# Sliding-window attention and a token-mixing MLP on one core: ScalarE's transpose copies as 4-byte words, part-wise waits, 20 output buffers, and 17 stores held back

## Chip, cores and metric

The kernel runs on one core of one Trainium2 chip. The core's engines are TensorE (PE in the profile, PEld for its weight loads), VectorE (DVE), ScalarE (ACT), GpSimd (POOL) and SyncE (SP), each with a queue of its own that runs in order and waits on semaphores. DMAs are issued from POOL (loads), SP (stores, three of the first loads) and ACT (three first loads, two last stores). The metric is the device time of one execution, in microseconds (us).

## What is computed

The reference, cut to its core. The batch is 8, heads 8, sequence 576, head size 64; all inputs and the output are float32.

```
scores = (q @ k.T) / sqrt(64) - slope[h] * |i - j|      # slope = 2 ** -(h + 1)
mask   = (i - j >= 0) & (i - j < 128)
attn   = softmax(where(mask, scores, -1e9))
x      = (attn @ v), heads side by side                   # (8, 576, 512)
wq, wk = x @ w_q, x @ w_k                                 # (8, 576, 64)
W      = wq @ wk.T / sqrt(64)                             # (8, 576, 576)
out    = relu(W @ x) @ w_out                              # (8, 576, 512)
```

## The kernel before, in words

The work is cut into small operations, and their order on every engine is a table of words, `ORDER` (lines 49 to 118). A word such as `QK2.1.0:P2` is an operation's name and its engine: P is PE, with the PSUM pair (and half) that it writes, A is ACT, D is DVE, G is POOL, S is SP. `Order.follow` reads the table, and the kernel emits each operation in that order (lines 1037 to 1041). A tile framework adds the waits between engines.

The names that this text uses, with batch b, query group g (0 to 3, of 128 rows each; the last 64 rows of a batch are its tail) and half u of the heads:

- Loads on POOL: `Lq`, `Lk`, `Lv`, and `Lt` (the tails of two batches). They read float32 and write float16.
- `TQb`, `TKb.m`, `TTb`, `TJ` on PE transpose q, k and the tails into PSUM as float16; `ETQ`, `ETK`, `ETT`, `EJ` copy the result into the tile `qkT` (two of them, for batch b % 2), on ACT or DVE as the table says.
- `QKb.g.u` on PE makes scores, `EXPb.g.u` on ACT their exponential (line 657), `MULb.g` on DVE multiplies by mask and distance bias (line 672).
- `PVb.t` on PE multiplies by v, `RCb.t` and `Xb.t` on DVE divide by the sums: x, 128 rows at a time (t = 4 is the tail).
- `XTb.i` and `XTT` on PE transpose x; `EXTb.i` and `EXTT` copy it into the tile `xT` or `xTt`, on ACT or DVE.
- The MLP goes by groups of two batches (`GROUPS`): `WQ`, `WK`, `WT`, `G`, `MX` on PE with their evictions `EWQ`, `EWK`, `EWT`, `EG`, `RM`, `RMT`, then `OUTb.st` on PE, `EOb.st` on ACT or DVE (a copy from PSUM into an output buffer `osb`), and `DOb.st`, the store of 256 KB from that buffer. The last block of all, 7.3, is done in two halves, a and b.

Every copy goes through `cp` (lines 250 to 254): `scalar.copy` on ACT (L252 in the profile), `tensor_copy` on DVE (L254). All matmuls are recorded at L240, transposes at L243. Output buffers come from one pool of `OSB = 14` (line 35); the first three loads of q and k use three of them too. An `EO` needs a free buffer, which means that the store which read it has landed. The stores are nearly all on SP's queue, in the order of the table; the first, DO3.3, stands there behind EO3.3, and the stores of groups 0 and 1 (batches 0 to 3) follow it, each between other words.

The framework tracks whole regions of a tile: two operations of different engines that write interleaved pieces of one tile can be made to wait for each other. `apart` (lines 258 to 271) takes such waits away between the two halves of a PSUM pair.

Of the kernel before, what the change touches and what calls it, by code (L numbers as in the profile page):

```python
# [34 lines left out]
OSB = 14  # L35

GROUPS = ((0, 1), (2, 3), (4, 5), (6, 7))

LOGB = ()
# [27 lines left out]
Lk3.3:G QK2.0.1:P1 X1.4:D EXT0.1:D QK2.1.1:P0 Lk3.2:G EXP2.0.1:A TT2:P3 QK2.1.0:P2 ETT2:D
Lv2.1:G EXP2.1.1:A ETT3:D WK0:P10 MUL2.0:D Lv2.2:G EXP2.1.0:A XTT0:P0 QK2.3.0:P3 EXTT0:D
WQ0:P11 Lv2.3:G EWK0:A MUL2.1:D EXP2.3.0:A QK2.3.1:P0 TQ3:P2 Lq4.0:G MUL2.2:D EXP2.3.1:A Lwo0:G
WT0:P10 ETQ3:D PV2.0:P0 EWT0:A Lwo1:G TK3.0:P3 ETK3.0:A G0:P10 RC2.0:D Lk4.1:G X2.0:D MUL2.3:D  # L70
EWQ0:A Lk4.0:G TK3.1:P3 EG0:A QK3.0.0:P0 EXP3.0.0:A Lv3.0:G ETK3.1:D MX0.0:P1 QK3.0.1:P2
RM0.0:D MX0.1:P3 EXP3.0.1:A Lv3.1:G MX0.3:P0 Lq5.01:G RM0.3:D RM0.1:A PV2.1:P1 QK3.1.0:P2
RC2.1:D PV2.2:P3 EXP3.1.0:A X2.1:D MX0.2:P0 RC2.2:D QK3.3.1:P1 RM0.2:A X2.2:D PV2.3:P2 Lq5.02:G
MUL3.0:D QK3.1.1:P3 EXP3.3.1:A XT2.0:P00 PV2.4:P01 RC2.3:D EXP3.1.1:A Lq5.03:G X2.3:D TQ4:P1
RC2.4:D EXT2.0:A X2.4:D QK3.2.1:P3 ETQ4:D OUT0.2:P20 Lq5.00:G EXP3.2.1:A XT2.1:P21 Lv3.2:G
MUL3.1:D EO0.2:A QK3.2.0:P1 TK4.0:P3 Lv3.3:G EXP3.2.0:A QK3.3.0:P0 ETK4.0:D OUT0.1:P20 Lk5.0:G
EXT2.1:D EXP3.3.0:A QK4.0.1:P1 MUL3.2:D QK4.1.1:P3 Lk5.1:G OUT1.3:P21 EXP4.1.1:A Lv3.4:G
MUL3.3:D PV3.0:P0 EO0.1:A PV3.1:P3 Lk4.3:G EXP4.0.1:A OUT1.1:P20 RC3.1:D RC3.0:D X3.1:D Lk4.2:G
EO1.3:A QK4.1.0:P1 X3.0:D TQ5:P3 EXP4.1.0:A Lt2:G MX0.4:P0 XT3.0:P21 ETQ5:D RMT0:A PV3.2:P1
EO1.1:A PV3.3:P0 Lv5.0:G RC3.2:D EXT3.0:A X3.2:D OUT1.2:P20 Lv4.0:G RC3.3:D X3.3:D QK4.0.0:P1  # L80
TK5.0:P3 Lv4.1:G EXP4.0.0:A XT3.1:P21 ETK5.0:D PV3.4:P00 Lk5.3:G EO1.2:A QK5.1.0:P3 RC3.4:D
QK5.0.1:P1 X3.4:D EXP5.1.0:A OUT0.0:P20 Lv4.2:G EXT3.1:D MUL4.0:D EXP5.0.1:A QK5.0.0:P0 Lk5.2:G
TK4.1:P3 OUT0.3:P21 EXP5.0.0:A Lk6.0:G ETK4.1:D TT4:P1 EO0.0:D EO0.3:A Lq6.02:G XTT2:P3
QK5.1.1:P0 ETT5:D ETT4:A OUT1.0:P20 EXTT2:D Lk6.2:G EXP5.1.1:A MUL4.1:D PV4.0:P3 Lk6.1:G
# [6 lines left out]
MX2.0:P3 RC5.1:D PV4.3:P0 Lq7.01:G X5.1:D RM2.0:A QK5.3.1:P2 RC4.3:D TQ6:P1 Lv5.2:G X4.3:D
EXP5.3.1:A MX2.1:P3 ETQ6:D QK5.3.0:P0 Lq7.03:G RM2.1:A XT4.1:P20 Lq7.00:G PV4.4:P21 EXT4.1:D
EXP5.3.0:A TK7.0:P1 QK6.1.0:P3 Lv5.4:G ETK7.0:D OUT3.3:P20 EXP6.1.0:A RC4.4:D Lv5.3:G X4.4:D
QK6.1.1:P1 MUL5.2:D QK6.2.1:P0 QK6.2.0:P3 Lv7.3:G EXP6.1.1:A OUT2.1:P21 Lk7.2:G EXP6.2.0:A
XT5.0:P10 OUT2.3:P11 Lk7.3:G EO2.1:A EXT5.0:D EXP6.2.1:A MUL5.3:D PV5.2:P3 Lv6.2:G OUT2.2:P10
EO3.3:A Lv6.0:G RC5.2:D EO2.3:A DO3.3:S X5.2:D TT6:P2 EO2.2:A TQ7:P0 Lv6.1:G DO0.2:S ETT6:D
QK6.0.1:P3 ETT7:D DO2.1:S QK6.0.0:P1 ETQ7:D Lv6.3:G EXP6.0.1:A PV5.4:P20 DO0.1:S OUT3.2:P21
DO1.3:S Lv6.4:G EXP6.0.0:A RC5.4:D DO1.0:S MUL6.1:D QK6.3.0:P0 Lv7.0:G DO0.0:S PV5.3:P3
EXP6.3.0:A OUT3.1:P10 X5.4:D Lv7.4:G RC5.3:D EO3.2:A X5.3:D Lv7.2:G QK6.3.1:P0 EO3.1:A
QK7.1.0:P2 MUL6.0:D MX2.4:P3 EXP6.3.1:A XT5.1:P11 Lv7.1:G OUT2.0:P10 RMT2:D EXP7.1.0:A EXT5.1:D  # L100
TK7.1:P0 QK7.0.0:P3 EO2.0:A XTT4:P2 MUL6.2:D OUT3.0:P11 EXTT4:A EXP7.0.0:A ETK7.1:D WT4:P10
QK7.1.1:P2 MUL6.3:D EWT4:A QK7.0.1:P3 PV6.0:P0 EXP7.1.1:A WK4:P10 RC6.0:D X6.0:D EXP7.0.1:A
# [57 lines left out]
def kernel(  # L160
# [75 lines left out]
    def hold(i):  # L236
        held.append(i.ins)
# [12 lines left out]
    def cp(eng, out_ap, in_ap):  # L250
        if eng == "ACT":
            hold(nc.scalar.copy(out_ap, in_ap))  # L252
        else:
            hold(nc.vector.tensor_copy(out=out_ap, in_=in_ap))  # L254
# [820 lines left out]
```

## Time and profile before

| | us |
|---|---|
| runs shown | 136.86, 137.61, 137.75 (median 137.61) |
| the profiled execution | 138.33 |
| its span, first to last instruction | 136.6 |
| busy: PE / DVE / ACT / POOL | 124.7 / 114.1 / 107.5 / 86.3 |
| weight loads on PE (PEld) | 79.3 |

The span is what the trace shows; 1.7 us of the profiled execution lie around it. Of an engine's row in a timeline, the first number is the start from the beginning of the span, the second the time, and the brackets hold how long the engine was idle just before and what ended that. In groups of instructions by line, the numbers behind the bar are busy time, mean nanoseconds of one, and idle time ahead of them. A wait for several semaphores is put down to the one that came last.

### The profile page before, as it was taken

How to read it: one execution, taken by the hardware profiler on the slowest of the kernel's cores; microseconds unless marked ns; L12 is line 12 of the kernel's file. 1: busy time of each engine (PE TensorE's matmuls, PEld its weight loads, DVE VectorE, ACT ScalarE, POOL GpSimd, SP SyncE). 2: the span in 40 equal slices, each digit the busy share in tenths (PEclk: the TensorE clock that was granted, in tenths of full speed). 3: DMA queues.
4: the chain of work that ended last, by engine and by line, in shares of the span. 5: the costliest groups of instructions: out<-in, count | busy, mean ns of one | idle time of the engine just before them, and what ended most of it. 6: DMA issues, size and time to landing. Idle time of an engine off the chain costs nothing.

```text
span 136.6 us, 5058 instructions
## 1 busy us (share of the span) xinstructions
PE 124.7 (91%) x2176; PEld 79.3 (58%) x2176; DVE 114.1 (84%) x197; ACT 107.5 (79%) x145; POOL 86.3 (63%) x108
## 2 busy tenths in 40 slices
PE   6889668999999799999999999998999999999980
PEld 2456447676667476575566675564586476643440
DVE  5747979699999999998999999699899999557730
ACT  2579977896898999998999999997999971457030
POOL 7998969599969949899999999996000000000000
PEclk9999965899999999999999999999999999999999
DMA  4999999999999999999999999999999910759894
GB/s 100 216 176 168 157 154 184 160 156 154 151 159 165 196 181 153 157 154 156 155 157 157 153 150 149 150 198 229 240 233 323 321 58 5 236 180 349 257 366 154
DMA packets 105414, 24.97 MB, mean 183 GB/s; under 512 B 95536, under 2 KB 100912, under 8 KB 105392
## 3 DMA queue, kind: packets, MB, share of 16 engines
q0 software_dynamic: 96832, 14.42, 149.0%
q1 hardware_dynamic: 6688, 9.44, 20.5%
q10 hardware_dynamic: 1872, 0.79, 2.2%
q8 instruction: 17, 0.28, 0.8%
q14 instruction: 5, 0.04, 0.1%
HBM read 29.62 MB, written 9.44 MB: 286 GB/s over the span
## 4 chain that ended last, share of the span: by engine, by line
PE 49%; DMA 18%; POOL 10%; DVE 8%; ACT 8%; issue 3%; ACTq 0%; POOLq 0%; DVEq 0%
PE pair L240 41%; DMA natq<-in_q_dram 11%; PE pair L243 8%; DMA natk<-in_k_dram 6%; POOL natk L367 5%; ACT pt L657 4%; DVE qkT L254 2%; DVE pt L672 2%; POOL vt L393 2%; DVE rm L888 1%; DVE x L733 1%; POOL natt L387 1%; ACT qkT L252 1%; POOL natq L371 1%; POOL wqk_sb L455 1%
## 5 line engine op out<-in xcount | busy, mean ns | idle before, releaser
L657 ACT ACTIVATE pt<-pair 128x1024 f16<-128x1024 f32 x64 | 63.1, 1036 | 6.5 <-PE pair L240 6.0
L672 DVE TENSOR_TENSOR pt<-pt,bias 128x2048 f16<-128x2048 f16 x32 | 38.5, 1215 | 0.7 <-ACT pt L657 0.7
L393 POOL DMA_DIRECT2D vt<-in_v_dram x40 | 35.5, 980 | 0.7 <-DMA natq<-in_q_dram 0.4
L240 PE MATMUL pair<-wout_sb,rm 128*128 128x512 f16 (+1 forms) x132 | 31.7, 373 | 0.4 <-ACT osb L252 0.4
L367 POOL DMA_DIRECT2D natk<-in_k_dram x31 | 28.8, 956 | 2.0 <-DMA natq<-in_q_dram 1.5
L240 PEld LDWEIGHTS <-pt 128*128 128x128 f16 (+1 forms) x576 | 19.9, 103 | 6.6 <-issue 2.7
L240 PE MATMUL pair<-vt,pt 128*128 128x65 f16 (+1 forms) x576 | 22.9, 198 | 0.8 <-DVE rm L888 0.5
L240 PE MATMUL pair<-qkT 64*128 64x256 f16 (+2 forms) x320 | 22.6, 253 | 0.9 <-DVE qkT L254 0.5
L252 ACT COPY osb<-pair 128x512 f32<-128x512 f32 (+1 forms) x24 | 14.0, 597 | 11.3 <-PE pair L240 9.7
L733 DVE TENSOR_TENSOR x<-pair,inv 128x512 f16<-128x512 f32 x32 | 21.8, 690 | 0.9
L254 DVE COPY qkT<-pair 128x1024 f16<-128x1024 f16 (+2 forms) x27 | 19.3, 734 | 3.6 <-PE pair L243 3.5
L240 PEld LDWEIGHTS <-rm 128*128 128x128 f16 x132 | 11.4, 97 | 12.5 <-issue 2.7
L240 PEld LDWEIGHTS <-qkT 64*128 64x128 f16 x320 | 11.1, 94 | 8.8 <-issue 5.4
L379 POOL DMA_DIRECT2D natq<-in_q_dram x12 | 11.6, 1005 | 2.1 <-PE pair L240 1.4
L254 DVE COPY osb<-pair 128x512 f32<-128x512 f32 (+1 forms) x13 | 8.7, 667 | 5.1 <-PE pair L240 5.1
L886 ACT ACTIVATE rm<-pair 128x1024 f16<-128x1024 f32 x11 | 11.1, 1046 | 0.5 <-PE pair L240 0.3
L243 PE MATMUL pair<-identh,x 128*128 128x128 f16 x128 | 10.2, 225 | 0.4 <-ACT pt L657 0.4
L243 PEld LDWEIGHTS <-x 128*128 128x128 f16 x128 | 8.0, 100 | 2.7 <-issue 1.6
L240 PE MATMUL pair<-warm 128*128 128x512 f16 x24 | 8.1, 454 | 1.6 <-DVE warm L295 1.2
L254 DVE COPY xT<-pair 128x1024 f16<-128x1024 f16 x11 | 7.5, 685 | 1.9 <-PE pair L243 1.7
L243 PE MATMUL pair<-identh,natk 64*128 64x64 f16 x248 | 7.1, 194 | 2.0 <-DMA natk<-in_k_dram 0.8
L243 PEld LDWEIGHTS <-natk 64*128 64x128 f16 x248 | 5.6, 96 | 4.7 <-issue 2.8
(68 smaller groups left out, 135.9 us busy)
## 6 DMA issues: line engine op xcount, KB each, us to landing
out_dram<-osb SPq DMA_DIRECT2D x30, 256.0 KB, 3.4
vt<-in_v_dram POOLq DMA_DIRECT2D x32, 128.0 KB, 7.5
natk<-in_k_dram POOLq DMA_DIRECT2D x31, 128.0 KB, 6.0
natq<-in_q_dram POOLq DMA_DIRECT2D x4, 512.0 KB, 7.7
natq<-in_q_dram POOLq DMA_DIRECT2D x12, 128.0 KB, 5.6
out_dram<-osb SPq DMA_DIRECT2D x9, 128.0 KB, 2.5
vt<-in_v_dram POOLq DMA_DIRECT2D x8, 64.0 KB, 5.7
natt<-in_q_dram POOLq DMA_DIRECT2D x4, 128.0 KB, 5.6
```

Of the source, the lines that this page charges most:

```text
L240: hold(nc.tensor.matmul(*a, **k))
L243: hold(nc.tensor.transpose(*a))
L252: hold(nc.scalar.copy(out_ap, in_ap))
L254: hold(nc.vector.tensor_copy(out=out_ap, in_=in_ap))
L367: return lambda: nc.gpsimd.dma_start(out=natk(b, n), in_=k[b, :, P * n:P * n + P, :].transpose([1, 0, 2]))
L371: return lambda: nc.gpsimd.dma_start(out=natq_s[b % NQ][r0 // QR:P].rearrange("p h r d -> p h (r d)"), in_=q[b, :, r0:512, :].rearrange("h ...
L379: return lambda: nc.gpsimd.dma_start(out=rows_q(b)[:, r], in_=q[b, :, 0:512, :].rearrange("h (p r) d -> r p h d", r=QR)[r])
L393: return lambda: nc.gpsimd.dma_start(out=vtv(b, t)[:n, :, 0:D], in_=v[b, :, P * t:P * t + n, :].transpose([1, 0, 2]))
L657: nc.scalar.activation(out=pt, in_=two(hold_.bank).rearrange("p e c -> p (e c)"), func=AF.Exp, scale=SCALE)
L672: nc.vector.tensor_tensor(out=pv, in0=pv, in1=bt, op=ALU.mult)
L733: nc.vector.tensor_tensor(out=x_s[b % NX][qt].rearrange("p (g h d) -> p g h d", g=2, h=4), in0=sums(p)[:, :, :, 0:64], in1=box["inv"].unsq ...
L886: hold(nc.scalar.activation(out=out_ap, in_=in_ap, func=AF.Relu, scale=WSCALE))
```

## The change

1. `cp` on ACT: where source and destination are both float16, both are read as float32 words, so that one element holds two values.
2. `parts` is new, and `apart` calls it: for operations that touch `qkT` and `xT` it drops the framework's waits between engines and adds waits for the operations on which this one depends and for the earlier users of its PSUM banks.
3. `OSB` is 20 in place of 14.
4. In `ORDER` the words `DO` of the 17 first stores stand together behind EO3.0, DO3.0 first. Without the words `DO`, the table is the same before and after, word for word.
5. `LOGB`, which was empty, goes, with the branches that it would have switched on.

```diff
-OSB = 14
+OSB = 20
...
-LOGB = ()
...
-EO2.3:A DO3.3:S X5.2:D TT6:P2 EO2.2:A TQ7:P0 Lv6.1:G DO0.2:S ETT6:D
+EO2.3:A X5.2:D TT6:P2 EO2.2:A TQ7:P0 Lv6.1:G ETT6:D QK6.0.1:P3 ETT7:D QK6.0.0:P1 ETQ7:D Lv6.3:G
...
-PV6.1:P2 MUL7.1:D PV6.2:P0 EO3.0:A QK7.3.0:P3 EWK4:A RC6.2:D DO3.0:S RC6.1:D WQ4:P11 X6.2:D
+PV6.2:P0 EO3.0:A DO3.0:S DO0.2:S DO0.1:S DO1.3:S DO1.1:S DO1.2:S DO0.0:S DO0.3:S DO1.0:S DO1.4:S
+DO2.1:S DO3.3:S DO2.3:S DO2.2:S DO3.2:S DO3.1:S DO2.0:S QK7.3.0:P3 EWK4:A RC6.2:D RC6.1:D WQ4:P11
...
     def cp(eng, out_ap, in_ap):
         if eng == "ACT":
+            if out_ap.dtype == F16 and in_ap.dtype == F16:
+                out_ap, in_ap = out_ap.bitcast(FP32), in_ap.bitcast(FP32)
             hold(nc.scalar.copy(out_ap, in_ap))
...
+    PARTS = {"QK": "q", "EF": "q", "EJ": "q", "ETQ": "q", "ETK": "q", "ETT": "q", "EXT": "x"}
+    user, freed = {}, {}
+
+    def parts(op):
+
+        halves = [(op.bank[0], h) for h in range(2)] if op.banks == 2 else [op.bank] if op.banks else []
+        before = [o for x in halves for o in (user.get(x), *freed.get(x, ()))]
+        for x in halves:
+            user[x], freed[x] = op, []
+        for f in op.frees:
+            for h in range(2):
+                freed.setdefault((f.bank[0], h), []).append(op)
+        if op.kind in PARTS:
+            tile_ = PARTS[op.kind] + str(op.batch % (2 if PARTS[op.kind] == "q" else NX))
+            near = [d for d in (*op.deps, *before) if d is not None and d.insts]
+            keep = [i for d in near for i in d.insts]
+            for d in near:
+                if d.eng != op.eng:
+                    tc.add_manual_dep(held[0], d.insts[-1].name,
+                                      mybir.DependencyInfo(mybir.DependencyClass.Sync, mybir.DependencyReason.DATA),
+                                      reason="the parts it uses")
+            for i in held:
+                for e in KIND:
+                    if e != op.eng:
+                        tc.declare_no_dep(i, group=f"parts{tile_}{e}", keep=keep, reason="another part of the tile")
+                tc.add_to_no_dep_group(f"parts{tile_}{op.eng}", i)
+
     def apart(op):
...
         op.insts = list(held)
+        parts(op)
...
-            ps = two((bi or o).bank)
+            ps = two(o.bank)
```

**On ACT, from EXP6.3.0 to EXTT4.** The rows are, in turn, EXP6.3.0, EO3.2, EO3.1, EXP6.3.1, EXP7.1.0, EO2.0 and EXTT4, with the semaphores that each waits for; DMAHW0 to DMAHW7 tell of landed loads and stores of SP and ACT. Before:

```order
L657 ACTIVATE pt_101<-pair_140 128x1024 [waits DVE_49,PE_49]
L252 COPY osb<-pair_142 128x512 [waits DMAHW5_49,DMAHW3_49]
L252 COPY osb<-pair_141 128x512 [waits DMAHW6_49,PE_49,Activation_49]
L657 ACTIVATE pt_101<-pair_140 128x1024 [waits PE_49]
L657 ACTIVATE pt_103<-pair_142 128x1024 [waits DVE_49,PE_49]
L252 COPY osb<-pair_141 128x512 [waits DMAHW7_49,PE_49]
L252 COPY xTt_126<-pair_142 128x512 [waits PE_49]
```

And with the change:

```order
L654 ACTIVATE pt_99<-pair_138 128x1024 [waits DVE_49,PE_49]
L245 COPY osb<-pair_140 128x512
L245 COPY osb<-pair_139 128x512 [waits PE_49]
L654 ACTIVATE pt_99<-pair_138 128x1024 [waits PE_49]
L654 ACTIVATE pt_101<-pair_140 128x1024 [waits DVE_49,PE_49,Activation_49]
L245 COPY osb<-pair_139 128x512 [waits PE_49]
L245 COPY xTt_124<-pair_140 128x256 [waits PE_49]
```

The order of the instructions is the same. The three copies into `osb` no longer wait for a DMA, and the copy into `xTt` has 256 elements of a partition in place of 512.

**On SP, the first eight stores.** The number behind `osb` tells the buffers' uses apart; before, they are those of DO3.3, DO0.2, DO2.1, DO0.1, DO1.3, DO1.0, DO0.0 and DO3.0:

```order
L993 DMA out_0_dram<-osb_2050 128x512
L993 DMA out_0_dram<-osb_1221 128x512
L993 DMA out_0_dram<-osb_2024 128x512
L993 DMA out_0_dram<-osb_1286 128x512
L993 DMA out_0_dram<-osb_1316 128x512
L993 DMA out_0_dram<-osb_1577 128x512
L993 DMA out_0_dram<-osb_1537 128x512
L993 DMA out_0_dram<-osb_2384 128x512
```

With the change they are those of DO3.0, DO0.2, DO0.1, DO1.3, DO1.1, DO1.2, DO0.0 and DO0.3:

```order
L987 DMA out_0_dram<-osb_2375 128x512
L987 DMA out_0_dram<-osb_1219 128x512
L987 DMA out_0_dram<-osb_1284 128x512
L987 DMA out_0_dram<-osb_1314 128x512
L987 DMA out_0_dram<-osb_1390 128x512
L987 DMA out_0_dram<-osb_1469 128x512
L987 DMA out_0_dram<-osb_1535 128x512
L987 DMA out_0_dram<-osb_1537 128x512
```

The store of block 3.0, eighth before, is first, and as SP runs in order the others stand behind its wait for EO3.0. DO3.2, which stood among the stores of group 2 before, is one of the 17.

More of the change, by code (lines that the diff above doesn't have):

```diff
@@ L67 @@
[L67 to L84, printed above, removed]
@@ L91 @@
[L91 to L102, printed above, removed]
@@ new lines @@
+Lv2.0:G RC0.4:D PV1.4:P00 ETK2.0:D EXP2.2.0:A XT1.1:P20 Lk3.0:G RC1.4:D X0.4:D QK2.0.0:P3 EXT1.1:D
+XT0.1:P21 EXP2.0.0:A Lk3.3:G QK2.0.1:P1 X1.4:D EXT0.1:D QK2.1.1:P0 Lk3.2:G EXP2.0.1:A TT2:P3
+QK2.1.0:P2 ETT2:D Lv2.1:G EXP2.1.1:A ETT3:D WK0:P10 MUL2.0:D Lv2.2:G EXP2.1.0:A XTT0:P0 QK2.3.0:P3
+EXTT0:D WQ0:P11 Lv2.3:G EWK0:A MUL2.1:D EXP2.3.0:A QK2.3.1:P0 TQ3:P2 Lq4.0:G MUL2.2:D EXP2.3.1:A
+Lwo0:G WT0:P10 ETQ3:D PV2.0:P0 EWT0:A Lwo1:G TK3.0:P3 ETK3.0:A G0:P10 RC2.0:D Lk4.1:G X2.0:D
+MUL2.3:D EWQ0:A Lk4.0:G TK3.1:P3 EG0:A QK3.0.0:P0 EXP3.0.0:A Lv3.0:G ETK3.1:D MX0.0:P1 QK3.0.1:P2
@@ new lines @@
+EXP6.0.1:A PV5.4:P20 OUT3.2:P21 Lv6.4:G EXP6.0.0:A RC5.4:D MUL6.1:D QK6.3.0:P0 Lv7.0:G PV5.3:P3
+EXP6.3.0:A OUT3.1:P10 X5.4:D Lv7.4:G RC5.3:D EO3.2:A X5.3:D Lv7.2:G QK6.3.1:P0 EO3.1:A QK7.1.0:P2
+MUL6.0:D MX2.4:P3 EXP6.3.1:A XT5.1:P11 Lv7.1:G OUT2.0:P10 RMT2:D EXP7.1.0:A EXT5.1:D TK7.1:P0
+QK7.0.0:P3 EO2.0:A XTT4:P2 MUL6.2:D OUT3.0:P11 EXTT4:A EXP7.0.0:A ETK7.1:D WT4:P10 QK7.1.1:P2
+MUL6.3:D EWT4:A QK7.0.1:P3 PV6.0:P0 EXP7.1.1:A WK4:P10 RC6.0:D X6.0:D EXP7.0.1:A PV6.1:P2 MUL7.1:D
+PV6.2:P0 EO3.0:A DO3.0:S DO0.2:S DO0.1:S DO1.3:S DO1.1:S DO1.2:S DO0.0:S DO0.3:S DO1.0:S DO1.4:S
@@ new lines @@
+DO2.1:S DO3.3:S DO2.3:S DO2.2:S DO3.2:S DO3.1:S DO2.0:S QK7.3.0:P3 EWK4:A RC6.2:D RC6.1:D WQ4:P11
+X6.2:D EXP7.3.0:A X6.1:D PV6.4:P10 EWQ4:A QK7.3.1:P0 RC6.4:D QK7.2.1:P2 X6.4:D QK7.2.0:P3 EXP7.3.1:A
+MUL7.0:D G4:P11 EXP7.2.1:A MUL7.3:D PV6.3:P0 EG4:A OUT3.4:P10 EXP7.2.0:A RC6.3:D X6.3:D PV7.4:P11
+EO3.4:A MX4.4:P2 MX4.1:P3 RC7.4:D MX4.0:P0 X7.4:D RMT4:A XT6.0:P10 RM4.1:D RM4.0:A OUT5.4:P11
+EXT6.0:D MX4.2:P0 EO5.4:A XTT6:P3 MX4.3:P2 MUL7.2:D EXTT6:A XT6.1:P10 RM4.3:A WT6:P11 RM4.2:D
+PV7.2:P3 EXT6.1:A PV7.3:P2 EWT6:D OUT4.2:P00 RC7.2:D X7.2:D PV7.0:P1 OUT5.3:P01 RC7.3:D RC7.0:D
```

116 lines of the change are left out of this document (49 added, 67 removed).

## The prediction

> **What bounds the kernel now.** I read the busy time by stretch first, then the chain of waits, then each engine's timeline at the places that the change touches.
>
> ```profile
> 41.70:115.30 73.60, 71.55 (x1408) 46.59 (x1401) 69.96 (x116) 66.36 (x92) 50.31 (x60) 1.00 1.89 177
> 97.00:132.00 35.00, 35.00 (x481) 20.51 (x480) 27.60 (x47) 21.83 (x34) 0.00 (x0) 1.00 0.83 229
> ```
>
> The columns are length, then busy time of PE, PEld, DVE, ACT and POOL, granted clock, DMA share, GB/s. From 41.7 to 115.3 us three engines are nearly full: PE idles 2.05 us, DVE 3.64 us, ACT 7.24 us. DVE's work is not shortened by the change, so 3.64 us is the most that this stretch can give. From 97 to 132 PE is never idle.
>
> Before 41.7 us the chain of waits says this:
>
> ```profile
> 32.60 7.88 DMA natq<-in_q_dram
> 40.49 0.04 issue
> 40.53 1.08 PE pair L243 x32
> ```
>
> The load of batch 3's q lands at 40.5, and the 32 transposes TQ3 start on it. It was issued by POOL, whose only long idle time between 20 and 41 us is ended by the landing of an earlier load:
>
> ```profile
> L367 POOL DMA_DIRECT2D natk<-in_k_dram x8 | 7.1, 903 | 1.7 <-DMA natq<-in_q_dram 1.5 <-issue 0.2
> 41.66 1.22 DVE L254 COPY qkT<-pair 128x2048 f16<-128x2048 f16 x1
> ```
>
> DVE's copy ETQ3 at 41.66 follows TQ3's end (40.53 + 1.08 = 41.61). So all engines meet at that landing: time won ahead of it is lost there, and loads set it, not ACT.
>
> **The copies, in themselves.** Thirteen ACT copies move f16 to f16 and become copies of half as many f32 words:
>
> ```profile
> L252 ACT COPY osb<-pair 128x512 f32<-128x512 f32 x23 | 13.6, 607 | 10.6 <-PE pair L240 9.7 <-DMA out_dram<-osb 0.9
> L252 ACT COPY xT<-pair 128x1024 f16<-128x1024 f16 x5 | 5.1, 1028 | 0.0
> L252 ACT COPY qkT<-pair 128x512 f16<-128x512 f16 x4 | 2.1, 597 | 0.2 <-DVE qkT L254 0.2
> L252 ACT COPY qkT<-pair 128x2048 f16<-128x2048 f16 x1 | 1.9, 1900 | 0.0
> L252 ACT COPY xTt<-pair 128x512 f16<-128x512 f16 x2 | 1.2, 589 | 0.0
> L252 ACT COPY qkT<-pair 128x1024 f16<-128x1024 f16 x1 | 1.0, 1012 | 0.1
> L252 ACT COPY osb<-pair 128x256 f32<-128x256 f32 x1 | 0.4, 373 | 0.7 <-DVE osb L254 0.7
> ```
>
> At 512 elements f32 (607 ns) and f16 (597) cost the same, so the count of elements sets the time. 2048 to 1024 elements saves 1900 - 1012 = 0.88 us; 1024 to 512 saves about 0.42, six times, 2.5 us; 512 to 256 saves 597 - 373 = 0.22, six times, 1.3 us. Together 4.7 us of ACT. The trace has no f32 copy in short strided pieces; the bounds are no saving (the f16 price stays) and 4.7 us. I take the saving, since the two flat rows are nearest.
>
> **Where that time goes.** Five copies stand ahead of 40.5 us (ETT0, ETT1, EJ0.3.1, ETQ2, EXT1.0, 1.96 us): worth 0. ACT's idle time behind the first three says so too, as it does behind EXT3.0 later:
>
> ```profile
> 23.31 1.56 ACT L252 COPY qkT<-pair 128x512 f16<-128x512 f16 x3
> 25.34 1.02 ACT L657 ACTIVATE pt<-pair 128x1024 f16<-128x1024 f32 x1 [0.46 <-PE pair L240]
> 60.63 1.04 ACT L252 COPY xT<-pair 128x1024 f16<-128x1024 f16 x1
> 62.27 1.02 ACT L657 ACTIVATE pt<-pair 128x1024 f16<-128x1024 f32 x1 [0.59 <-PE pair L240]
> ```
>
> After EXT3.0 (60.63) ACT waits for PE already; a shorter copy makes that wait longer. ETK3.0 and EXT2.0, the two left between 41.7 and 60 us, stand ahead of instructions (EG0, EXP3.2.1) whose matmuls PE ends just as ACT gets there; I take 0 for each, with 0.42, the whole copy, as the upper bound if PE's results were there earlier.
>
> One copy in the middle is on the path, ETT4:
>
> ```profile
> 67.38 0.58 ACT L252 COPY qkT<-pair 128x512 f16<-128x512 f16 x1 [0.24 <-DVE qkT L254]
> 67.86 1.03 ACT L657 ACTIVATE pt<-pair 128x1024 f16<-128x1024 f32 x1
> 68.94 0.39 PE L240 MATMUL pair<-qkT 64*128 64x256 f16 x4 [0.28 <-ACT pt L657]
> ```
>
> QK4.2.1 waits for the exponential behind it, EXP5.1.1. ETT4's own wait of 0.24 us, for ETT5 on DVE, stays. 0.22 us less there starts PE 0.2 us earlier, and from there PE and ACT take turns without slack until 84 us. DVE idles little in between, so I count **0.2 us**, bounds 0 and 0.22.
>
> The other four (EXTT4, EXTT6, EXT6.1, EXT7.1, 1.3 us) lie behind 96.9 us, where PE has no idle time to remove: 0, covered by PE's own work; without that cover 1.3.
>
> **The exact waits.** Four copies lose one wait each, for the other engine's copy into another part of the tile (EJ0.2.1, ETK3.1, EXT3.1, EXT6.1). The one in the chain is ETK3.1's:
>
> ```profile
> 42.74 1.01 ACT qkT L252
> ...
> 44.77 0.68 DVE qkT L254
> ```
>
> ETK3.0 on ACT ended at 43.75, and DVE came to ETK3.1 at 44.77, a microsecond later: the wait cost nothing. PE's added wait, of QK3.0.0 for ETQ3, asks for a copy that ended at 41.66 + 1.22 = 42.88, before ETK3.0, which PE waits for anyway. The removed LOGB branches issued no instruction. All of it 0; a wait that held DVE back would be worth at most DVE's idle 3.64.
>
> **Buffers and stores.** This is the main term.
>
> ```profile
> 92.67 0.58 ACT L252 COPY osb<-pair 128x512 f32<-128x512 f32 x1
> 92.14 1.02 PE L240 MATMUL pair<-wout_sb,rm 128*128 128x512 f16 x4
> 94.11 0.58 ACT L252 COPY osb<-pair 128x512 f32<-128x512 f32 x1 [0.86 <-DMA out_dram<-osb]
> 94.59 1.95 ACT L657 ACTIVATE pt<-pair 128x1024 f16<-128x1024 f32 x2
> 94.75 1.02 PE L240 MATMUL pair<-wout_sb,rm 128*128 128x512 f16 x4 [0.36 <-ACT osb L252]
> 96.59 0.29 PE L243 MATMUL pair<-identh,xtl 64*128 64x64 f16 x8 [0.26 <-ACT pt L657]
> 97.40 1.22 DVE L672 TENSOR_TENSOR pt<-pt,bias 128x2048 f16<-128x2048 f16 x1
> 99.30 0.21 DVE L723 RECIPROCAL inv<-pair 128x8 f32<-128x8 f32 x1 [0.68 <-PE pair L240]
> ```
>
> EO3.1 (94.11) idles ACT 0.86 us until a store leaves its buffer. Behind it stand two exponentials; PE waits for EO3.1's bank (OUT2.0, 94.75) and for the second exponential's (XTT4, 96.59); DVE then waits 0.68 for PV6.0. With 20 buffers EO3.1 waits for no store; its input, OUT3.1, ends at 92.14 + 1.02 = 93.16, so it starts 0.86 earlier, right behind EO3.2, and so do the exponentials and XTT4. DVE can give only the 0.68 that it idled, and PE has a little slack against DVE behind it. I take **0.8 us**, bounds 0.68 and 0.86.
>
> The stores and the loads share the DMA engines:
>
> ```profile
> vt<-in_v_dram POOLq DMA_DIRECT2D x6, 128.0 KB, 5.8
> ...
> out_dram<-osb SPq DMA_DIRECT2D x7, 256.0 KB, 8.2
> vt<-in_v_dram POOLq DMA_DIRECT2D x6, 128.0 KB, 10.5
> PEld L240 <- DMA vt<-in_v_dram: 0.2, 1, 0.2
> ```
>
> The first row is from 70 to 87 us, the next two from 88 to 94.5, when seven stores run: loads of v take 10.5 us instead of 5.8. PE waited for only one of them, by 0.2 us, at PV5.4. With stores held until EO3.0 is done that wait goes; half of it reaches OUT3.1: **0.1 us**, bounds 0 and 0.2.
>
> What is queued behind the held store: all 39 DMA issues of SP, and through buffers EO4.3 and later. EO4.3 runs at 115.5 and needs the first held store, EO4.2 the second, and so on, about one a microsecond.
>
> ```profile
> 100.88 0.59 ACT L252 COPY osb<-pair 128x512 f32<-128x512 f32 x1
> DMA packets 1112, 2.00 MB, mean 286 GB/s; under 512 B 145, under 2 KB 145, under 8 KB 1110
> q1 hardware_dynamic: 6688, 9.44, 20.5%
> 115.52 0.59 ACT L252 COPY osb<-pair 128x512 f32<-128x512 f32 x1 [3.88 <-PE pair L240]
> ```
>
> The first row is EO3.0; 0.86 earlier it ends at 100.6, and the stores start there. Seventeen are 17 of 36 equal parts of 9.44 MB, 4.46 MB; at 286 GB/s (104 to 111 us, mostly stores) 15.6 us, so the first lands near 104 and the last near 117. Each buffer is free some ten microseconds before it is wanted. Cost 0, bounds 0 and rival (4).
>
> **Sum.** 0.2 + 0.8 + 0.1 = 1.1 us on PE; DVE, which must deliver X7.1 to XT7.0 near 115 us, gives back about 1.0. The profiled execution took 138.33 us (span 136.6): 137.3, span 135.6. The median of the runs shown, 137.61, lies 0.72 below that execution: 137.61 - 1.0 = **136.6 us**.
>
> **Rivals.**
> (1) *DVE replaces the wait.* PE and ACT gain, DVE's queue does not; for it speak 69.96 busy of 73.60. Against it: the 0.68 us idle at 99.30 is ended by PE. Time: 0.2 us gained, 137.4.
> (2) *ACT was the bound throughout.* All 4.7 us would come out, cut by DVE's idle time to 3.64: 134.0. Against it stand ACT's own waits for PE, quoted above.
> (3) *The tail is not PE's own.* PE's records overlap, so a full row need not mean a full engine; if copies gate it after 97 us, the 1.3 us come out as well: 137.61 - 1.0 - 1.3 = 135.3. For it: weight loads fill only 20.51 of 35.00 us. Against it: no PE wait is recorded there, and ACT waits 3.88 us for PE at 115.52.
> The Trainium skill (Perfetto Trace Analysis, Identifying the Most-Contended Engine) says that matmul occupancy is no fair measure of PE's headroom and that weight-load share and MFU are; by that rule PE has room after 97 us and this rival wins. The row of weight loads fits the rule; the wait of ACT for PE speaks for the other reading.
> (4) *The store queue becomes the bound: slower.* Now all 9.44 MB must leave between 100.6 and the end. If 17 stores at once, and those behind them, ran at the 229 GB/s that all DMAs averaged from 97 to 132 us, the last would land at 100.6 + 41.2 = 141.8 instead of within the span of 135.6, 6.2 us later: 136.6 + 6.2 = 142.8. It decides from 9.44 MB in 135.6 - 100.6 = 35 us, 270 GB/s, downwards. Against it: the 286 GB/s of 104 to 111 us, with the queue running dry in its last slices.
>
> **How the numbers follow.** Chances: forecast 0.50, (1) 0.20, (2) 0.08, (3) 0.12, (4) 0.10. The forecast's own range, from the bounds of its terms, is 136.0 to 137.1. A change of 1% (1.4 us) is about what a measurement of this kernel can tell. Faster by more than that: (2), (3) and a quarter of the forecast, 0.33; slower: 0.10; the rest, 0.57, within. The range reaches to (1) with half a microsecond of spread and to (3): 135.2 to 137.9, leaving out (2) and (4).
>
> **What would show it.** Right: no ACT wait for a store near 94 us, XTT4 at about 95.5, DVE's idle time before RC6.0 gone, loads of v landing in under 7 us after 88 us, the 32 transposes of TQ3 still at 40.5 us, f16 copies at about half their time, PE full from 96 us. Wrong: TQ3 earlier than 40 us, ACT waiting for stores after 115 us, or a last store that lands long after PE's end.

## The result, and the profile after

The changed kernel takes 136.62 us (median of 16 runs, 135.69 to 137.9); the kernel before, run beside it, 137.57 us (16 runs, 136.6 to 138.37). The ratio is 0.9942, with a 95% interval of 0.9919 to 0.9966: 0.8 us faster, more than nothing by its interval and less than the 1% that the prediction takes as what a measurement of this kernel can tell. (It compares undisturbed runs alone, and so stands a little nearer to 1 than the two medians, which are 0.95 us apart.) The forecast was 136.6. The profiled execution of the changed kernel took 136.26 us, 2.07 less than that of before, of which only part is the change, as the runs below show.

The busy time by stretch of the changed kernel; the second row is the tail, 2.4 us earlier than the one shown of before:

```profile
41.70:115.30 73.60, 72.24 (x1385) 46.56 (x1382) 70.32 (x117) 64.35 (x91) 48.67 (x57) 1.00 1.90 184
94.60:129.60 35.00, 35.00 (x481) 20.49 (x480) 28.41 (x48) 20.63 (x34) 0.00 (x0) 1.00 0.82 252
```

PE and DVE hold the middle as before (1.36 and 3.28 us idle), ACT now idles 9.25 us instead of 7.24, and in the tail PE is as full as it was. ScalarE's copies, by form:

```profile
L245 ACT COPY xT<-pair 128x512 f32<-128x512 f32 x5 | 3.0, 602 | 0.0
L245 ACT COPY qkT<-pair 128x256 f32<-128x256 f32 x4 | 1.3, 378 | 0.3 <-DVE qkT L247 0.2
L245 ACT COPY qkT<-pair 128x1024 f32<-128x1024 f32 x1 | 1.0, 1020 | 0.0
L245 ACT COPY xTt<-pair 128x256 f32<-128x256 f32 x2 | 0.8, 376 | 0.0
L245 ACT COPY qkT<-pair 128x512 f32<-128x512 f32 x1 | 0.6, 585 | 0.1
```

The thirteen take 6.7 us where they took 11.3: 4.6 less, against 4.7 forecast, and the short strided pieces cost nothing extra. ACT around the place of the old wait for a store, then PE, then DVE:

```profile
91.19 1.11 ACT L245 COPY osb<-pair 128x512 f32<-128x512 f32 x2
92.21 1.95 ACT L654 ACTIVATE pt<-pair 128x1024 f16<-128x1024 f32 x2
94.03 0.61 ACT L245 COPY osb<-pair 128x512 f32<-128x512 f32 x1
94.53 0.37 ACT L245 COPY xTt<-pair 128x256 f32<-128x256 f32 x1
```

```profile
92.28 0.62 PE L234 MATMUL pair<-identh,x 128*128 128x128 f16 x8
92.74 1.03 PE L231 MATMUL pair<-wout_sb,rm 128*128 128x512 f16 x4
94.20 0.29 PE L234 MATMUL pair<-identh,xtl 64*128 64x64 f16 x8
```

```profile
97.06 0.20 DVE L717 RECIPROCAL inv<-pair 128x8 f32<-128x8 f32 x1
```

EO3.2 and EO3.1 (91.19, two copies) run back to back. From XT5.1 (92.28) to XTT4 (94.20) it is 1.92 us; before, with XT5.1 in the row below, it was 96.59 - 93.77 = 2.82: 0.90 us less, in two steps, 0.52 at OUT2.0 and 0.38 at XTT4.

```profile
93.77 0.62 PE L243 MATMUL pair<-identh,x 128*128 128x128 f16 x8
```

DVE's 0.68 us idle before RC6.0 is gone. At ETT4 the same comparison gives the other step, ACT first and PE behind it:

```profile
66.11 0.37 ACT L245 COPY qkT<-pair 128x256 f32<-128x256 f32 x1 [0.24 <-DVE qkT L247]
66.38 1.03 ACT L654 ACTIVATE pt<-pair 128x1024 f16<-128x1024 f32 x1
```

```profile
67.01 0.85 PE L231 MATMUL pair<-qkT 64*128 64x256 f16 x8
```

QK4.2.0 and QK4.2.1 now stand in one row without idle time between them; QK4.2.1 begins at 67.46, 0.45 us behind QK4.2.0, where before it began 0.67 behind it. These two steps, 0.21 and 0.90, are all that differs between the two profiles from 46 us to the end (1.1 us together). Ahead of 46 us the profile of the changed kernel leads by another 1.27 us, and its TQ3 starts at 39.09, not at 40.5. The loads of v issued while no store runs:

```profile
vt<-in_v_dram POOLq DMA_DIRECT2D x6, 128.0 KB, 5.4
```

Before, the same six took 10.5 us, beside seven stores.

Three questions are open from this. Is the early 1.27 us the change's? The wait that went, 0.86 us: was it there in every execution? And what is the hold for, if the step that I gave it (0.1 us at PV5.4) is not to be seen?

### The profile page after: what moved, and what is told of

It reads as the page before. It is cut to its first block, busy times and chain, and to the rows that moved or that the text cites. A ratio compares the mean times of both kernels' runs of the same rounds, so it can differ in the third digit from the quotient of the medians.

```text
span 134.2 us, 5053 instructions
## 1 busy us (share of the span) xinstructions
PE 122.3 (91%) x2176; PEld 77.2 (58%) x2176; DVE 114.1 (85%) x197; ACT 103.2 (77%) x145; POOL 86.3 (64%) x108
## 3 DMA queue, kind: packets, MB, share of 16 engines
q1 hardware_dynamic: 6688, 9.44, 20.7%
HBM read 29.62 MB, written 9.44 MB: 291 GB/s over the span
## 4 chain that ended last, share of the span: by engine, by line
PE 59%; DMA 16%; DVE 9%; ACT 6%; POOL 3%; issue 3%; ACTq 0%; POOLq 0%; DVEq 0%
PE pair L231 48%; DMA natq<-in_q_dram 12%; PE pair L234 11%; DMA natk<-in_k_dram 4%; ACT pt L654 4%; DVE pt L666 3%; DVE qkT L247 3%; DVE rm L882 2%; POOL natk L378 1%; DVE x L727 1%; ACT rm L880 1%; POOL vt L404 1%; POOL natq L382 1%; ACT wqT L245 0%; ACT gs L245 0%
## 5 line engine op out<-in xcount | busy, mean ns | idle before, releaser
L231 PE MATMUL pair<-vt,pt 128*128 128x65 f16 (+1 forms) x576 | 22.2, 194 | 2.2 <-DVE pt L666 0.6
L231 PEld LDWEIGHTS <-pt 128*128 128x128 f16 (+1 forms) x576 | 19.2, 100 | 8.0 <-issue 3.5
L231 PE MATMUL pair<-qkT 64*128 64x256 f16 (+2 forms) x320 | 22.1, 250 | 0.4 <-DVE qkT L247 0.2
L231 PEld LDWEIGHTS <-qkT 64*128 64x128 f16 x320 | 10.6, 94 | 8.3 <-issue 2.8
L390 POOL DMA_DIRECT2D natq<-in_q_dram x12 | 11.1, 949 | 1.8 <-PE pair L231 1.6
L234 PEld LDWEIGHTS <-x 128*128 128x128 f16 x128 | 7.5, 98 | 2.3 <-issue 1.3
L234 PE MATMUL pair<-identh,natq 128*64 128x128 f16 (+2 forms) x256 | 6.9, 206 | 0.9 <-DMA natq<-in_q_dram 0.9
```

The source lines that it names most:

```text
L231: hold(nc.tensor.matmul(*a, **k))
L234: hold(nc.tensor.transpose(*a))
L390: return lambda: nc.gpsimd.dma_start(out=rows_q(b)[:, r], in_=q[b, :, 0:512, :].rearrange("h (p r) d -> r p h d", r=QR)[r])
```

## The experiments

All times of the table below are from one profile of each kernel. "Landing" is that of the last load of q of batch 5 (Lq5.00), "v 6.4" that of the last v block of batch 6; the three differences are the places at which the profiles part: QK4.2.0 to QK4.2.1, XT5.1 to XTT4, and PV6.1 to QK7.3.1 (PV6.4 lies in between). The last column is the time from TQ5 to the start of the last matmuls, OUT7.3a.

| kernel | landing | TQ5 | QK4.2 | to XTT4 | v 6.4 | to QK7.3.1 | TQ5 to end |
|---|---|---|---|---|---|---|---|
| before | 58.11 | 58.63 | 0.67 | 2.82 | 100.16 | 2.63 | 73.31 |
| before, again | 59.43 | 59.47 | 0.66 | 1.97 | 102.27 | 2.63 | 72.41 |
| words alone | 58.18 | 58.23 | 0.45 | 2.21 | 101.63 | 3.20 | 72.96 |
| buffers alone | 57.13 | 57.18 | 0.67 | 1.92 | 100.34 | 3.04 | 72.71 |
| all but the hold | 58.70 | 58.75 | 0.45 | 1.92 | 101.56 | 2.90 | 72.36 |
| buffers and hold alone | 57.95 | 57.99 | 0.66 | 1.92 | 95.78 | 2.63 | 72.34 |
| no hold, v of batch 6 first | 57.53 | 57.58 | 0.45 | 1.92 | 97.43 | 2.63 | 72.09 |
| the change | 57.38 | 57.43 | 0.45 | 1.92 | 95.87 | 2.63 | 72.13 |
| tail copies as f16 | 57.51 | 57.56 | 0.45 | 1.92 | 96.22 | 2.63 | 72.10 |
| without part-wise waits | 58.51 | 58.56 | 0.45 | 1.92 | 96.56 | 2.63 | 72.07 |

The last column adds up to within 0.1 us: 72.1, and what the three columns have above 0.45, 1.92 and 2.63. "Words alone" is 72.1 + 0.29 + 0.57 = 72.96; "buffers alone" 72.1 + 0.22 + 0.41 = 72.73. Four runs told below are not in the table; three of them have 0.45, 1.92 and 2.63 us in the three places and 72.07 to 72.17 in the last column, and the fourth is the one with ETT4 as f16.

### Before, once more

No edit.

> The kernel before, unchanged, timed against itself. It leaves out every part of the change. Theory (the change wins 0.2 us at QK4.2.1 and 0.9 us at OUT2.0 and XTT4, together 1.1 us, and the further 1.3 us by which the profiled execution of the changed kernel leads before 45 us belongs to the executions, not to the change): ratio 1.000, a profiled time of 136.6 to 138.4, and a landing of the q of batch 3 that lies anywhere between 38.6 and 40.5 us. In the stretch from MX0.1 to the end this kernel should take the same time as the profiled execution of before took, 2.4 - 1.3 = 1.1 us more than the changed kernel, to within 0.2. Rival (the early 1.3 us belong to the change, the words on ScalarE for instance): the landing stays at 40.5 us and QK1.3.0 starts near 24.8 us as in the first profile of before.

Measured: ratio 1.0011 (0.9971 to 1.0051), the profiled execution 138.55 us. The chain of waits and, from the timeline of ACT, the place of the old wait:

```profile
34.02 7.16 DMA natq<-in_q_dram
41.18 0.04 issue
41.22 0.80 PE pair L243 x21
```

```profile
93.44 1.16 ACT L252 COPY osb<-pair 128x512 f32<-128x512 f32 x2
```

The same kernel landed the q of batch 3 at 41.18 instead of 40.49, so this landing does wander. It came later than the 38.6 to 40.5 us that I had expected, though, so that both profiles of this kernel are late here: this run alone does not exclude the rival, and the next two do. And EO3.2 and EO3.1 ran back to back without a wait: the 0.86 us on which my main term rests is not there in this execution (1.97 us to XTT4). From TQ5 to the end it is slower than the changed kernel by 0.3 us (72.41 against 72.13), not by the 1.1 that I expected.

### The words alone

```diff
         if eng == "ACT":
+            if out_ap.dtype == F16 and in_ap.dtype == F16:
+                out_ap, in_ap = out_ap.bitcast(FP32), in_ap.bitcast(FP32)
             hold(nc.scalar.copy(out_ap, in_ap))
```

> Before, with the word copies alone: all thirteen of ScalarE's f16 copies as 4-byte words, 14 buffers, stores and waits as before. Theory: ScalarE does 4.7 us less, of which 0.2 us come out, all at QK4.2.1; ScalarE still waits 0.8 to 0.9 us for a store at EO3.1: ratio 0.998 to 0.999, 0.2 us. Rival 1 (ScalarE bounds the early part too, and the early 1.3 us come from its copies): ratio 0.989, 1.5 us. Rival 2 (all of ScalarE's saved time counts): ratio 0.974, 3.6 us.

Measured: 1.0001 (0.9968 to 1.0034). That excludes the rival by which all 4.7 us count (0.974), and an early gain of 1.5 us (0.989). The step of 0.21 at QK4.2.1 is there. ACT's wait for a store, expected at 0.8 to 0.9 us, is 0.24 this time, and PE has a wait that the first profile of before did not show; ACT, then PE:

```profile
92.78 0.59 ACT L254 COPY osb<-pair 128x512 f32<-128x512 f32 x1 [0.24 <-DMA out_dram<-osb]
```

```profile
101.10 0.20 PE L240 MATMUL pair<-vt,pt 128*64 128x65 f16 x2
101.67 0.41 PE L240 MATMUL pair<-vt,pt 128*64 128x65 f16 x14 [0.38 <-DMA vt<-in_v_dram]
```

This is PV6.4, the tail block of batch 6. Its v, issued at 90.24, landed at 101.63.

### The buffers alone

The changed kernel with the old order of stores, f16 copies and the old waits; against before:

```diff
-OSB = 14
+OSB = 20
```

> The changed kernel's 20 output buffers with the stores where they stood before, the copies as f16 and the waits as before: the buffers alone. Theory: EO3.1 waits for no store, OUT2.0 starts 0.5 us and XTT4 0.9 us earlier against what stands ahead of them, and the loads of v behind 88 us still take about 10 us as they share the DMA engines with seven stores: ratio 0.9935, 0.9 us. Rival 1 (the hold matters: with the stores among the loads a load or DVE takes the place of the wait): ratio 0.997 to 1.000. Rival 2 (EO3.1's wait costs nothing since DVE binds behind it): ratio 1.000.

Measured: 0.9985 (0.9960 to 1.0011). Theory said 0.9935, and that lies outside. The interval holds both rivals; the profile speaks for the first. The wait at EO3.1 is gone (1.92 us to XTT4), but PV6.4 waits, in the timeline of PE:

```profile
99.96 0.21 PE L236 MATMUL pair<-vt,pt 128*64 128x65 f16 x2
100.38 0.41 PE L236 MATMUL pair<-vt,pt 128*64 128x65 f16 x14 [0.21 <-DMA vt<-in_v_dram]
```

Everything ahead of PV6.4 comes sooner, its v does not (landed 100.34): 0.41 us go back behind PV6.1. In the profile of before PV6.4 started at 102.41, with its v landed at 100.16, since EO3.1's wait had held PE up; in the second one at 102.36, 0.09 us behind the landing. PE in the first profile of before:

```profile
102.41 0.42 PE L240 MATMUL pair<-vt,pt 128*64 128x65 f16 x16
```

### The change without the hold

The 17 words `DO` back where they stood before.

> The changed kernel with the 17 stores back where they stood before: word copies, part-wise waits and 20 buffers, without the hold. Theory: the hold is worth 0 (the step that I gave it, 0.1 us at PV5.4, does not show in the profile of the changed kernel): ratio against before 0.992, the same as the whole change (0.994) within 0.2 us. Rival 1 (the hold carries the gain through the loads): ratio 0.998 to 1.000. Rival 2 (the hold costs time at the end, since the stores crowd the tail): ratio 0.988 to 0.990, better than the whole change by 0.5 us or more.

Measured: 0.9983 (0.9953 to 1.0013), and 0.27 us lost at PV6.4, whose v landed at 101.56. PE there, and in the changed kernel:

```profile
101.31 0.70 PE L236 MATMUL pair<-vt,pt 128*64 128x65 f16 x16
```

```profile
100.02 0.43 PE L231 MATMUL pair<-vt,pt 128*64 128x65 f16 x16
```

The value that I had expected, 0.992, is excluded, and 1.0000 is not, which speaks for rival 1. The interval overlaps that of the whole change (0.9919 to 0.9966), so the times alone do not show what the hold is worth; the profile does.

### Buffers and hold, without words and part-wise waits

```diff
-            if out_ap.dtype == F16 and in_ap.dtype == F16:
-                out_ap, in_ap = out_ap.bitcast(FP32), in_ap.bitcast(FP32)
...
-        parts(op)
```

> The changed kernel without its word copies and part-wise waits: 20 buffers and the held stores alone. Theory as the first four runs leave it (stores that run among the loads cost time at one of two places: EO3.1 waits for a buffer, 0.9 us in the first profile of before and 0.24 in that of the words, or PV6.4 waits for its last load of v, 0.2 to 0.5 us; buffers cure the first, the hold the second): neither wait shows, Lv6.4 lands before 97 us, and the ratio is 0.995 to 0.996, the whole change less the 0.2 us of the words. Rival 1 (the words are needed for the gain, since ScalarE only then has room): 0.998 or more. Rival 2 (the hold alone does it all, the words nothing): 0.994.

Measured: 0.9962 (0.9935 to 0.9990), as the theory had it. Neither wait shows; the v of block 6.4 landed at 95.78. Only the 0.21 us at QK4.2.1 are missing against the change.

### No hold, but the v of batch 6 first

The kernel without the hold, with one word of `ORDER` moved, `Lv7.3`, from ahead of `Lk7.2` to behind `Lv6.4`:

```diff
-Lv7.3:G Lk7.2:G Lk7.3:G Lv6.2:G Lv6.0:G Lv6.1:G Lv6.3:G Lv6.4:G
+Lk7.2:G Lk7.3:G Lv6.2:G Lv6.0:G Lv6.1:G Lv6.3:G Lv6.4:G Lv7.3:G
```

(Other words between them are left out.)

> The kernel without the hold (words, part-wise waits, 20 buffers, stores where they stood before) with one load moved: that of v block 7.3 is issued behind the five blocks of batch 6, not ahead of them, so that those land one transfer, about 0.7 us, sooner. Theory (what the hold gives is the landing of block 6.4, for which PV6.4 waits): PV6.4's wait for the load goes, QK7.3.1 starts 0.3 to 0.4 us earlier against XTT4 than without the move, and the ratio is 0.995 to 0.996 in place of 0.998. Rival (the hold works by something else, the stores' start or ScalarE): the same as without the move, 0.998, though the block lands sooner.

Measured: 0.9957 (0.9927 to 0.9986). The block landed at 97.43 instead of 101.56. That is 4.1 us, where I had expected the 0.7 of one transfer: this execution was 1.2 us earlier throughout, and where the other 2.2 came from no run shows. PV6.4 starts without a wait:

```profile
100.14 0.42 PE L227 MATMUL pair<-vt,pt 128*64 128x65 f16 x16
```

So what the hold gives can be had without it: it is the landing of this load, and nothing that the stores do themselves. The two intervals (0.9953 to 1.0013 without the move) overlap; the step in the profile, 2.90 to 2.63 us, is the firmer evidence.

### Four tail copies as f16

EXTT4, EXTT6, EXT6.1 and EXT7.1 are left out of the word copies:

```diff
-            if out_ap.dtype == F16 and in_ap.dtype == F16:
+            if out_ap.dtype == F16 and in_ap.dtype == F16 and state["op"] not in PLAIN:
```

> The changed kernel with four of its word copies back as f16: EXTT4, EXTT6, EXT6.1 and EXT7.1, all behind 94 us, 1.3 us of ScalarE's time. Theory (the tail is TensorE's own): the same time as the whole change, ratio 0.994, with 0.0 to 0.2 us at EXTT4, which lies just ahead of the tail. Rival (3) of the prediction (ScalarE's copies gate the tail): 1.3 us more, ratio 1.003.

Measured: 0.9923 (0.9895 to 0.9951). ACT and the busy time of the tail:

```profile
106.94 0.59 ACT L247 COPY xTt<-pair 128x512 f16<-128x512 f16 x1
108.33 1.03 ACT L247 COPY xT<-pair 128x1024 f16<-128x1024 f16 x1
```

```profile
94.70:129.70 35.00, 35.00 (x481) 20.50 (x480) 28.42 (x48) 21.86 (x34) 0.00 (x0) 1.00 0.84 253
```

ACT does 1.23 us more than in the changed kernel (21.86 against 20.63), and of PE's operations behind 94 us only WT6 moves, by 0.03 us that are gone at OUT4.2: every other step to the end is the same to 0.01 us. So ScalarE's copies do not gate the tail.

### Stores held longer

First the block of 17 words was set behind EO5.4 in the table.

> The changed kernel with the 17 stores held longer, until the copy EO5.4 is done, some 8 us later: near 107 us instead of 99. It tests the price of rival (4). Theory: the store queue has room in the changed kernel (its last store lands 3.7 us behind PE's last start); held 8 us longer it becomes the bound: 17 stores took from 99.1 to 114.9 us, 283 GB/s, and at that rate 9.44 MB from 107 us end at 140, 6 us later than now: ratio 1.03 to 1.04. If the stores run at the 360 GB/s that the fullest slices of the profile show, they end at 133.5, no later than now: ratio 0.994 to 1.000. I expect between, 1.01 to 1.03. Rival (stores are free wherever they stand): 0.994.

Measured: 0.9959 (0.9927 to 0.9991). My edit missed its aim: SP's queue holds only stores by then, so words that move past other engines' words leave it as it is. DO3.0 was still first, and was issued at 99.77 as soon as EO3.0 was done. The run repeats the changed kernel, and with it (0.9942) it gives an idea of how well such a ratio repeats. Then the store of block 5.4 was set ahead of the 17:

```diff
-DO3.0:S DO0.2:S DO0.1:S
+DO5.4:S DO3.0:S DO0.2:S DO0.1:S
```

(all of them behind EO5.4).

> The changed kernel with SP's queue held until EO5.4 is done, near 107 us in place of 99: the store of block 5.4 is the first of the queue and the 17 follow it. (The run before it that was to do so moved words of the table and left SP's order as it was: DO3.0 was still the first, was issued at 99.8, and that run repeats the changed kernel.) Theory: held so long the queue is the bound of the end. In the changed kernel the stores land some 0.75 us apart (101.1 for the first, 112.1 for the sixteenth issue), about 350 GB/s; 9.44 MB at that rate take 27 us, so from 107.3 the last lands near 135 to 136 in place of 133.3: 1.5 to 3 us more than the changed kernel, ratio 1.005 to 1.016. At the 283 GB/s of all 17 it would be 140.7: ratio 1.045. Rival (the end is not set by the store queue even then): 0.994.

Measured: 1.0122 (1.0058 to 1.0185, from four runs), in the range that I had expected. The DMA view of this kernel from 107 us, and of the changed kernel from 99 us, each in 40 slices up to its end:

```profile
DMA  0029999996899999999998459999999999999400
GB/s 0 0 64 210 310 356 351 374 379 223 328 359 328 297 374 405 399 387 399 402 402 287 102 136 302 376 389 389 392 392 335 347 389 396 399 392 329 149 4 0
```

```profile
DMA  0999999967899994068668408989289999999800
GB/s 0 351 382 310 349 398 403 363 247 182 338 405 405 405 389 156 12 240 226 149 272 214 109 0 338 398 298 379 75 328 282 300 333 391 393 356 311 284 22 0
```

In the changed kernel the queue runs nearly dry several times between 112 and 124 us (12, 0 and 75 GB/s); held until 108.00, it does so less, once, near 125 us (102 GB/s). The last store landed at 137.99, 3.7 us later than in the changed kernel, of which PE's own delay in this execution, 1.03 us, is already taken off. PE, ACT and DVE go as in the changed kernel (72.07 us from TQ5). 9.44 MB from 108.00 to 137.99 are 315 GB/s.

### The q of batch 3 first

```diff
-Lk3.1:G EXP2.2.1:A Lw0:G RC0.3:D WM.5:P01 PV1.3:P2 EXT1.0:A X0.3:D Lq3.0:G
+EXP2.2.1:A Lw0:G RC0.3:D WM.5:P01 PV1.3:P2 EXT1.0:A X0.3:D Lq3.0:G Lk3.1:G
```

> The changed kernel with one load moved: that of k block 3.1 is issued behind the q of batch 3 and not ahead of it. Theory (the landing of the q of batch 3, and after it that of the q of batch 5, at which TQ5 starts in five of nine profiles, set the time up to 58 us; what TensorE, ScalarE and DVE do ahead of them is worth nothing): the q of batch 3 lands 0.5 to 0.9 us earlier relative to its issue, TQ3 starts earlier by up to that, and half or more of it is lost at TQ5, since the loads as a whole end no sooner: ratio 0.991 to 0.994. Rival (the landing of the q of batch 3 alone is the bound): 0.9 us less, ratio 0.988.

Measured: 0.9957 (0.9919 to 0.9994): no gain over the change (0.9942). The q of batch 3 landed at 37.96 and TQ3 started at 38.79, so that PE got there later than the load. MX0.1 was at 43.94, 0.3 us ahead of the changed kernel's profile, and then PE:

```profile
57.67 0.64 PE L230 MATMUL pair<-identh,natq 64*128 64x64 f16 x32 [0.51 <-DMA natq<-in_q_dram]
```

TQ5 waited for the load of the next q but one (Lq5.00, landed 57.62) and was 0.24 us behind that of the changed kernel.

### Without the part-wise waits

```diff
-        parts(op)
```

> The changed kernel without the part-wise waits: words, 20 buffers and held stores. Theory (the waits that go were never the last to end): from TQ5 to the end 72.1 us as in the changed kernel, ratio 0.994. Rival (a wait that goes was worth something, at ETK3.1 or EXT3.1): a step of 0.2 us or more between TK3.0 and TQ5 or at EXT3.1.

Measured: 0.9947 (0.9912 to 0.9981), 72.07 us from TQ5, no step anywhere between TK3.0 and the end but at TQ5, where PE waits 0.17 us for a landing. The waits are worth nothing.

### ETT4 alone as f16

```diff
+PLAIN = ("ETT4")
...
-            if out_ap.dtype == F16 and in_ap.dtype == F16:
+            if out_ap.dtype == F16 and in_ap.dtype == F16 and state["op"] not in PLAIN:
```

> The changed kernel with one copy, ETT4, back as f16. Theory: QK4.2.1 starts 0.21 us later behind QK4.2.0 than in the changed kernel (0.67 in place of 0.45 us) and nothing else moves, so that of the 4.7 us of the thirteen copies this one holds all that comes out: from TQ5 to the end 72.3 in place of 72.1 us, ratio 0.9955. Rival (the words count at more places): the step stays at 0.45 us, or a second step shows elsewhere.

Measured: 0.9967 (0.9932 to 1.0001). PE:

```profile
67.03 0.39 PE L233 MATMUL pair<-qkT 64*128 64x256 f16 x4
67.69 0.40 PE L233 MATMUL pair<-qkT 64*128 64x256 f16 x4 [0.27 <-ACT pt L656]
```

The step is back, 0.66 us, with twelve of thirteen copies still as words. From TQ5 it took 72.62 us: a second step of 0.21 stands at TK5.1, which started at 70.62, 0.04 us behind the landing of its k block 5.2 (70.58; 69.62 in the changed kernel). That is a load again, and not the copy.

## Why the prediction was right, and where its reasons were not

**The copies (0.2 us).** Right, in place and in size. The step of 0.21 us at QK4.2.1 is in all profiles with ETT4 as words, and missing in all without (0.66 to 0.67 against 0.45 us). One copy of thirteen holds it: 0.2 of 4.6 us. That the others are worth 0 holds too: there is no step behind ETK3.0, EXT2.0 and EXT3.0, and the tail copies are worth 0 by experiment.

**The exact waits (0).** Right.

**The buffers (0.8 us).** The mechanism was right: without the wait at EO3.1, OUT2.0 and XTT4 start 0.90 us earlier, as against 0.68 to 0.86 forecast. What failed was to take it for the kernel's and not for the execution's. With 14 buffers the loss at this place was 0.90, 0.05 and 0.29 us in three profiles. And where it is small, or is taken away by buffers, the next thing is late: PV6.4's load of v, for 0.57, 0.41 and 0.27 us in three of the four profiles that had stores among the loads and no long wait at EO3.1 (in the fourth, the second of before, PE came just late enough, 0.09 us behind the landing). I had looked for such a wait only where the profile of before had one (PV5.4, 0.2 us). At PV6.4 the numbers to read were the landing, 100.16, and the start, 102.41: a margin of 2.25 us, of which the 1.1 us that were to be won leave half, with a landing that came between 100.16 and 102.27 in the five profiles of that order of loads and stores.

**The hold (0.1 us).** Under-sized, and at the wrong place. PV5.4 gained nothing. The hold takes the loads of v from 10.5 to 5.4 us, and that keeps PV6.4 free of a wait: in the profiles that is 0.27 us of the changed kernel (2.90 against 2.63). In the times the whole change is at 0.9942 and the change without the hold at 0.9983, but their intervals overlap. Taken together, what I called 0.8 and 0.1 is one quantity: stores among loads cost some 0.6 us at one of two places (0.90, 0.05 and 0.29 + 0.57 = 0.86 in the three profiles with 14 buffers, mean 0.60); buffers alone move it, and buffers with the hold, or with the load issued sooner, remove it. With the 0.21 of ETT4 this gives 0.8 us, which is what was measured (0.8); my sum was 1.0. Three profiles that lie between 0.05 and 0.90 fix such a mean to some 0.3 us only, so that it comes out so exactly is in part luck. So is the forecast's 136.6 against 136.62: its main term was read from the one of three profiles in which that wait was long, and the losses at PV6.4, which the prediction did not have, make up for it in the mean. The range of 136.0 to 137.1 given with it does not follow from the bounds of the three terms either: 0.68 to 1.28 us would be 136.3 to 136.9.

The Trainium skill (DMA: Bandwidth & Descriptors, Queues, rings and completion order) says that a DMA engine takes turns between the queues that have work, packet by packet. The doubled time of the loads beside seven stores, 10.5 against 5.4 us, agrees with it; that the turns go packet by packet no run here shows.

**Ahead of 40.5 us (0).** The conclusion was right and the place too narrow. TQ3 started between 38.71 and 41.22 us; the sign "still at 40.5" was wrong, and by the text's own test ("TQ3 earlier than 40 us") something was amiss. What sets the time up to 58 us is the landing of loads, not of that one alone: in twelve of the thirteen profiles other than that of before, TQ5 starts 0.04 or 0.05 us behind the landing of Lq5.00 (0.12 in the thirteenth), and in four of them PE was there first and idled for it, 0.17 to 0.51 us; moving the q of batch 3 ahead was worth nothing. The 1.27 us between the two first profiles are of this kind. The medians leave no room for them: 0.8 us were measured, and 0.8 are accounted for behind 58 us. The other kernels say the same: the nine with 20 buffers and the old order of the first loads are on average at a ratio of 0.9958, 0.57 us below before, and their last column is 72.29 us on average, 0.67 below that of the three profiles with 14 buffers (72.96, with 0.21 put back for the words). In eleven profiles with 20 buffers TQ3 came at 39.3 on average, in three with 14 at 40.5; but those three are of executions longer than their kernels' medians (138.33, 138.55 and 138.13 us against 137.57, 138.2 and 137.36). Whether a part of it, up to some 0.3 us, belongs to the change stays open.

**The rivals.** (1) *DVE replaces the wait* (0.20): something did replace it, in the kernels with buffers and no hold, but a load and not DVE. (2) *ACT the bound* (0.08): excluded by the words alone, 1.0001. (3) *The tail is not PE's own* (0.12): excluded by the f16 copies in the tail, no lasting step behind 94 us. The rule cited with it, of the Trainium skill (Perfetto Trace Analysis, Identifying the Most-Contended Engine), reads weight loads at 20.49 of 35.00 us as room on TensorE; the measurement decides, and 1.23 us more work on ScalarE found cover behind PE all the same. (4) *The store queue* (0.10): not in this kernel. The queue reached 315 GB/s when it was pressed, where 270 were needed; held 9 us longer it is the bound, and the kernel 1.2% slower than before.

## What to carry to other kernels

A wait that one profile shows at the end of a chain of DMAs belongs to that execution until a second profile of the same kernel shows it: profile it twice before the wait is made the main term. When such a wait is to go, read for every load used behind it how far its landing lies ahead of its use, since what is won is won against those margins; here a load with 2.25 us to spare in one profile took up to 0.57 us back in others. A queue with one kind of work is held by what stands first in it, not by where its words stand among other engines' words.

## What the runs showed of the hardware

The granted clock of TensorE was at half rate from 17.96 to 24.78 us in the first profile of before, and for some 3.4 us of that stretch in three other profiles. Clock (the number behind PE, PEld, DVE, ACT and POOL) from 17 to 25 us, in before, in its second profile, and with ETT4 as f16:

```profile
17.00:25.00 8.00, 6.51 (x103) 4.79 (x102) 6.39 (x11) 6.10 (x8) 6.71 (x9) 0.57 2.12 170
```

```profile
17.00:25.00 8.00, 5.23 (x115) 3.61 (x113) 7.43 (x12) 7.30 (x9) 6.61 (x9) 1.00 1.92 147
```

```profile
17.00:25.00 8.00, 6.67 (x132) 5.16 (x129) 7.09 (x13) 6.32 (x10) 6.80 (x8) 0.79 2.10 169
```

PE took longer there: from the warm-up matmuls WM.2 to PV1.0, which spans the stretch, it took 10.38 us in before and 9.03 to 9.75 in the other three, against 8.48 to 9.15 in the ten profiles at full clock. Of this nothing is to be seen later: TQ3 started at 40.53, 41.22 and 39.11 us in the three shown, the latest at full clock, and TQ5 at 58.18 us on average in the three half-clock profiles with the old order of loads and at 58.08 in the ten. That fits the landing of loads as what sets the time up to 58 us. The second row has the lowest rate of the DMAs of all profiles, 147 GB/s, and it is that execution in which the loads, and with them all up to 58 us, came last.
